# Newton steps of the norms' reciprocal roots: thirteen short chains taken from VectorE to GpSimd

## The chip, the cores and the metric

The program runs on one core of a Trainium2 chip. Time is device time in microseconds (us) from the first to the last instruction of the program, plus a little around it; of several runs the median is given. The engines of the core work side by side, each through its own list of instructions in a fixed order: PE (TensorE, matmuls), PEld (its weight loads), DVE (VectorE), ACT (ScalarE), POOL (GpSimd) and SP (SyncE), which here issues all transfers.

## What is computed

Attention over 4 batches, 12 heads, 448 positions and head size 64, with RMS norms on q and k, followed by two feed-forward layers over 1792 tokens (768 to 2048 to 768 each).

```python
def rmsnorm(x, g):
    rms = np.sqrt(np.mean(x * x, axis=-1, keepdims=True) + 1e-06)
    return x / rms * g
...
q_n, k_n = (rmsnorm(q, g_q), rmsnorm(k, g_k))
scores = scale * np.matmul(q_n, k_n.transpose(0, 1, 3, 2))
...
attn = np.exp(scores)
...
h = x @ w_in
g = h * (1.0 / (1.0 + np.exp(-1.702 * h)))
return (g @ w_out).astype(np.float32)
...
h = x @ w_in
g = np.maximum(h, 0.0) + alpha * np.minimum(h, 0.0)
return (g @ w_out).astype(np.float32)
```

## The kernel before

Two heads make a pair; there are 6 pairs in a batch (`NP`) and 24 in all. Fp32 values are split into two fp16 parts (high and low), and three matmuls of parts stand for one of fp32. The weights come as 64-bit words and are put together, scaled and split on ACT and DVE (`from_words`, lines 132, 148 and 149; row maxima, line 222; splits, lines 163 and 164). `w1i` and `w1o` are the two weights of the first layer.

The head of a pair's work is `normalize` and `prep_pair`. In `normalize`, ACT squares q and k (line 365), DVE sums the squares (line 367) into `ss`, 14 sums per partition and pair, and a reciprocal root `rs` is made from `ss`: one addition (line 368), a seed by integer arithmetic on the bits (line 371), and three Newton steps of three instructions each (lines 375 to 377). These 11 instructions depend on each other in a row. Then q and k are multiplied by the gains (line 382) and by `rs` (line 383), on DVE for the first 8 pairs and on POOL for the other 16. `prep_pair` copies the result to fp16 on ACT (line 396), takes the rest as the low part (line 397, same choice of engine) and has both transposed by a transfer (`hl` to `t1`; for the first pairs `t1` lies in the space of `w1o`). Only then can PE make scores (line 446). `normalize` runs for pair 0, for pair 1, and then for two pairs at once: 13 times in all.

The program starts with half of the work of batch 0 for its 6 pairs (`first_pairs`: scores, exponents, transposes by matmuls on line 493, products with v on line 529), and takes three steps of `w1i` with each of its steps. When the row scales of `w1i` and the scale of v are known, `first_x` splits the attention's output (tile `x`, lines 124 and 125), and the first feed-forward matmuls start (line 624, tile `hp`), mixed with the other half of batch 0 and the steps of `w1o`. Their results go through lines 635 and 636 into `g0`, are split (line 125, tile `g`) and feed the first layer's second product (line 694, tile `yp`), the first of which stands where batch 0 is done. Then the batches follow each other, with the next batch's attention spread between the matmuls, and the second layer comes last.

The order of each engine is not the order of the code: a scheduler simulates the program with its own prices and lists each engine's instructions as they come ready. So short instructions of a dependent row can have others between them, and a change of a few instructions moves many others. SP's list is in order too: a transfer that waits holds up those behind it.

Of the kernel before, what the change touches and what calls it, by code (L numbers as in the profile page):

```python
# [14 lines left out]
ALU = mybir.AluOpType  # L15
# [41 lines left out]
def attention_moe_kernel(  # L57
# [17 lines left out]
    nc = tc.nc  # L75
# [277 lines left out]
    def normalize(*Ps):  # L353

        Ps = [P for P in Ps if P < B * NP]
        if not Ps:
            return
        n = NT2
        w = 2 * n * len(Ps)
        ss = small.tile([128, 4 * NT2], F32, tag="ss", name="ss")[:, 0:w]  # L360
        for t, P in enumerate(Ps):
            flat = raws[P].rearrange("p h c d -> p (h c) d")
            for i in range(2):
                sq = att_p.tile([128, n, D], F32, tag="sq", name="sq", bufs=SQB)
                nc.scalar.activation(out=sq, in_=flat[:, i * n:(i + 1) * n], func=AF.Square, scale=2.0 ** -13)
                o = (2 * t + i) * n
                nc.vector.tensor_reduce(out=ss[:, o:o + n], in_=sq, op=ALU.add, axis=AX)
        nc.vector.tensor_scalar(out=ss, in0=ss, scalar1=1e-6 * 2.0 ** -20, scalar2=None, op0=ALU.add)
        rs = small.tile([128, 4 * NT2], F32, tag="rs", name="rs")[:, 0:w]
        tn = small.tile([128, 4 * NT2], F32, tag="tn", name="tn")[:, 0:w]  # L370
        nc.vector.tensor_scalar(
            out=rs.bitcast(I32), in0=ss.bitcast(I32), scalar1=-0.5, scalar2=RSQRT_SEED, op0=ALU.mult, op1=ALU.add
        )
        for _ in range(3):
            nc.vector.scalar_tensor_tensor(out=tn, in0=rs, scalar=-0.5, in1=ss, op0=ALU.mult, op1=ALU.mult)
            nc.vector.tensor_tensor(out=tn, in0=tn, in1=rs, op=ALU.mult)
            nc.vector.scalar_tensor_tensor(out=rs, in0=tn, scalar=1.5, in1=rs, op0=ALU.add, op1=ALU.mult)
        for t, P in enumerate(Ps):
            side = nc.vector if P < NP + 2 else nc.gpsimd
            ks = raws[P][:, :, 0:4]  # L380
            flat = raws[P].rearrange("p h c d -> p (h c) d")
            side.tensor_tensor(out=ks, in0=ks, in1=gs.unsqueeze(1).to_broadcast([128, 2, 4, D]), op=ALU.mult)
            side.tensor_tensor(
                out=flat, in0=flat, in1=rs[:, 2 * n * t:2 * n * (t + 1)].unsqueeze(2).to_broadcast([128, 2 * n, D]), op=ALU.mult
            )
# [187 lines left out]
    def first_pairs():  # L573

        steps = attention([4 * P + r for P in range(NP) for r in range(2)])
        for i, _ in enumerate(steps):
            P, r = divmod(i, 2)
            if P >= NP:
                yield
                continue  # L580
            if r == 0:
                prep = prep_pair(P + 1) if P + 1 < NP else iter(())
            next(prep, None)
            if r == 0 and P % 2 == 0 and P + 2 < NP:
                normalize(P + 2, P + 3)
            if r == 1:
                if P + 1 + QKB < NP:
                    load_qk(P + 1 + QKB)
                if P + 3 < NP:
                    load_v(P + 3)  # L590
            yield

    def other_batches():
        for i, _ in enumerate(attention(list(range(4 * NP, NU)))):
            P, r = divmod(4 * NP + i, 4)
            if P < B * NP:
                if r == 0:
                    prep = prep_pair(P + 1)
                next(prep, None)
                if r == NORM_AT and P % 2 == 0:  # L600
                    normalize(P + 2, P + 3)
                if r == 2 and P % NP == NP - 2 and P // NP + 1 < B:
                    with tc.issue_after(moved[P].ins):
                        v_scale(P // NP + 1)
                if r == 3:
                    load_qk(P + 1 + QKB)
                    load_v(P + 3)
            yield
# [416 lines left out]
    if True:  # L1025
# [30 lines left out]
        )  # L1056
        next(w1i_steps)
        normalize(0)
        for _ in prep_pair(0):
            pass  # L1060
# [88 lines left out]
```

## Time and profile before

| | |
|---|---|
| median of 3 runs | 1225.83 us (1224.32 to 1228.76) |
| the profiled execution | 1228.48 us, its span 1226.7 us |
| PE busy | 1087.1 us, 89% of the span |
| DVE busy | 842.5 us, 69% |
| ACT busy | 707.7 us, 58% |
| POOL busy | 80.2 us, 7%, 54 instructions |
| mean granted clock of TensorE | 0.960 |

Shares are means over the whole program. A stretch in which one engine is busy all the time while the others idle is limited by that engine, whatever the mean says. A short instruction on DVE is listed with a longer duration than the time it keeps the next one waiting: the start of the next row shows that.

### The profile page before, as it was taken

To read this page: it belongs to the slowest core of one execution; us is meant where nothing else is said; L and a number is where in the kernel's file an instruction comes from. 1 tells how busy PE (TensorE), PEld (TensorE's weight loads), DVE (VectorE), ACT (ScalarE), POOL (GpSimd) and SP (SyncE) were. 2 spreads that over 40 slices of the span, in tenths; PEclk is the share of its full clock that TensorE was granted. 3 is DMA by queue.
4 is the path that set the end of the run, shared out by engine and by line. 5 is a ranking of instruction groups with operands and counts; after the bars stand their busy time and mean duration, and the time that the engine had idled before them with its cause. 6 is when DMAs were issued, how large, how long until landed. Compare 5 with 4: busy or idle time off the path is not lost.

```text
span 1226.7 us, 18612 instructions
## 1 busy us (share of the span) xinstructions
PE 1087.1 (89%) x6829; PEld 608.2 (50%) x6829; DVE 842.5 (69%) x1594; ACT 707.7 (58%) x1447; POOL 80.2 (7%) x54
## 2 busy tenths in 40 slices
PE   0537499967998997999999999799999999999998
PEld 0315277746543443545545545344444467666665
DVE  7998868899656787556662577649896343787451
ACT  3666677878467867558874445227666444565220
POOL 0000000033212221221000000000000000000000
PEclk9966799988999998999999999899999999999999
DMA  7955426566777766655643641266524214354111
GB/s 221 282 155 169 117 54 145 130 124 125 156 146 148 141 135 114 130 127 115 111 99 81 236 157 49 79 235 219 198 89 155 78 65 157 107 160 117 46 32 33
DMA packets 266539, 160.62 MB, mean 131 GB/s; under 512 B 188112, under 2 KB 249808, under 8 KB 266448
## 3 DMA queue, kind: packets, MB, share of 16 engines
q1 hardware_dynamic: 266448, 159.44, 50.1%
q8 instruction: 53, 0.87, 0.3%
q14 instruction: 38, 0.31, 0.1%
HBM read 92.02 MB, written 25.69 MB: 96 GB/s over the span
## 4 chain that ended last, share of the span: by engine, by line
PE 56%; DVE 20%; DMA 11%; ACT 6%; issue 5%; SPq 2%; ACTq 0%; DVEq 0%
PE op L942 16%; PE yp L694 13%; PE hp L671 8%; PE h L779 6%; PE xp L529 5%; PE sp L446 3%; PE hp L624 3%; PE tp L493 2%; DMA yr<-y_dram 2%; DVE nm L451 2%; DVE ph L504 2%; DMA w2raw<-in_moe_w_in_dram 2%; ACT pr L460 1%; DMA vst<-in_v_dram 1%; DVE g L125 1%
## 5 line engine op out<-in xcount | busy, mean ns | idle before, releaser
L694 PE MATMUL yp<-g,w1o 128*128 128x448 f16 x1152 | 231.3, 360 | 5.2 <-DVE t L680 2.3
L779 PE MATMUL h<-x,w2i 128*128 128x512 f16 (+1 forms) x1152 | 219.3, 352 | 3.0 <-ACT neg L786 2.9
L671 PE MATMUL hp<-x,w1i 128*128 128x448 f16 x864 | 171.1, 355 | 3.0 <-DVE t L680 2.3
L694 PEld LDWEIGHTS <-w1o 128*128 128x128 f16 x1152 | 111.8, 99 | 116.9 <-issue 19.9
L779 PEld LDWEIGHTS <-w2i 128*128 128x128 f16 x1152 | 112.6, 98 | 108.6 <-issue 4.0
L671 PEld LDWEIGHTS <-w1i 128*128 128x128 f16 x864 | 82.7, 98 | 86.4 <-issue 12.8
L460 ACT ACTIVATE pr<-sp,nm,c_s 128x448 f32<-128x448 f32 x168 | 120.3, 720 | 4.9 <-PE tp L493 1.6
L504 DVE SCALAR_TENSOR_TENSOR ph<-pr,sm,ph 128x448 f16<-128x448 f32 x126 | 101.7, 831 | 25.0 <-ACT ph L478 24.9
L451 DVE TENSOR_REDUCE nm<-sp 128x2 f32<-128x896 f32 x96 | 92.7, 965 | 4.7 <-PE sp L446 4.4
L446 PE MATMUL sp<-t 64*128 64x448 f16 (+1 forms) x480 | 63.5, 370 | 29.7 <-ACT pr L460 13.5
L942 PEld LDWEIGHTS <-even 128*128 128x128 f16 x672 | 65.7, 98 | 43.1
L478 ACT ACTIVATE ph<-pr,sm 128x448 f16<-128x448 f32 x126 | 77.9, 661 | 14.5 <-DVE sm L469 14.1
L787 DVE SCALAR_TENSOR_TENSOR pos<-neg,nalpha,pos 128x512 f32<-128x512 f32 (+1 forms) x64 | 43.5, 682 | 60.0 <-ACT neg L786 59.9
L785 ACT ACTIVATE pos<-h 128x512 f32<-128x512 f32 (+1 forms) x64 | 34.5, 539 | 69.9 <-PE h L779 58.5
L624 PE MATMUL hp<-x,w1i 128*128 128x256 f16 (+1 forms) x576 | 64.3, 270 | 8.3 <-DVE t L636 7.5
L446 PE MATMUL sp<-w1o 64*128 64x448 f16 (+1 forms) x96 | 16.2, 462 | 62.0 <-DMA w1o<-hl 55.7
L942 PEld LDWEIGHTS <-odd 128*128 128x128 f16 x504 | 49.3, 98 | 32.6
L452 ACT ACTIVATE nm<-nm,c_s 128x2 f32<-128x2 f32 x96 | 28.0, 292 | 63.7 <-DVE nm L451 63.2
L942 PE MATMUL op<-w2lo,even 128*128 128x384 f16 x384 | 63.5, 326 | 0.0
L624 PEld LDWEIGHTS <-w1i 128*128 128x128 f16 x576 | 54.0, 102 | 18.8 <-issue 14.8
L125 DVE SCALAR_TENSOR_TENSOR g<-t,ratio_w1o,g 128x448 f16<-128x448 f32 x64 | 47.2, 741 | 16.0 <-ACT g L124 15.8
L493 PE MATMUL tp<-dg,pr 128*128 128x128 f32 x336 | 51.4, 308 | 5.1 <-DVE dg L473 3.8
(201 smaller groups left out, 1621.0 us busy)
## 6 DMA issues: line engine op xcount, KB each, us to landing
g<-in_moe_w_in_dram SPq DMA_DIRECT2D x24, 512.0 KB, 5.4
g<-in_moe_w_out_dram SPq DMA_DIRECT2D x32, 384.0 KB, 3.5
w2raw<-in_moe_w_in_dram SPq DMA_DIRECT2D x24, 512.0 KB, 5.8
w2raw<-in_moe_w_out_dram SPq DMA_DIRECT2D x16, 768.0 KB, 6.3
g_dram<-pos SPq DMA_DIRECT2D x48, 256.0 KB, 2.0
gp<-g_dram SPq DMA_DIRECT2D x8, 1024.0 KB, 7.6
odd<-g_dram SPq DMA_DIRECT2D x6, 1024.0 KB, 5.8
y_dram<-y SPq DMA_DIRECT2D x24, 224.0 KB, 2.4
```

The costliest lines, as they stand in the source:

```text
L446: nc.tensor.matmul(out=sp[:, j, 0:S] if n == 2 else sp[ds, 0, 0:S], lhsT=qt[ds] if n == 2 else qt[ds, 64:128], rhs=kt[ds, 0:S], start=(i = ...
L451: nc.vector.tensor_reduce(out=nm[:, 0:n], in_=sp[:, 0:n, 0:S], op=ALU.max, axis=AX, negate=True)
L460: nc.scalar.activation(out=pr[i], in_=sp[:, i, 0:S], func=AF.Exp, bias=nm[:, i:i + 1], scale=c_s, accum_out=sm[:, i:i + 1])
L478: nc.scalar.activation(out=ph[:, i, 0:S], in_=pr[i], func=AF.Copy, scale=sm[:, i:i + 1])
L493: nc.tensor.matmul(out=tp[:, c, i], lhsT=pr[i][:, o:o + 128], rhs=ph[:, i], start=True, stop=True)
L504: nc.vector.scalar_tensor_tensor(out=ph[:, i, S:2 * S], in0=pr[i], scalar=sm[:, i:i + 1], in1=ph[:, i, 0:S], op0=ALU.mult, op1=ALU.subtract)
L529: nc.tensor.matmul(out=xp[64 * j:64 * j + 64, t:t + n], lhsT=vs[ks, j, c], rhs=pt[ks, kc, o:o + n], start=(i == 0), stop=(i == len(steps) ...
L624: nc.tensor.matmul(out=ps, lhsT=w1i[:, kk, e, m * 128:(m + 1) * 128], rhs=xs[0, kk][:, f, cols], start=(i == 0), stop=(i == 3 * KD - 1))
L671: nc.tensor.matmul(out=ps, lhsT=w1i[:, kk, e, m * 128:(m + 1) * 128], rhs=x[:, f], start=(n == 0), stop=(n == 3 * KD - 1))
L694: nc.tensor.matmul(out=ps, lhsT=w1o[:, m, e, j * 128:(j + 1) * 128], rhs=g[:, m, f], start=(n == 0), stop=(n == 3 * KF - 1))
L779: nc.tensor.matmul(out=ps, lhsT=w2i[:, kk, e, m * 128:(m + 1) * 128], rhs=x2[kk][:, f], start=(c == 0), stop=(c == 3 * KD - 1))
L942: nc.tensor.matmul(out=ps, lhsT=ops[:, o, m, f], rhs=rhs[:, e], start=(c == 0), stop=(c == 3 * KH - 1))
```

## The change

The 11 instructions on DVE become 14 on POOL. POOL gets the addition and the seed as they are; a Newton step, three instructions with two operations each where that was possible, becomes four with plain products. The number of steps, the tiles and everything around them stay as they were.

```diff
-        nc.vector.tensor_scalar(out=ss, in0=ss, scalar1=1e-6 * 2.0 ** -20, scalar2=None, op0=ALU.add)
+        nc.gpsimd.tensor_scalar(out=ss, in0=ss, scalar1=1e-6 * 2.0 ** -20, scalar2=None, op0=ALU.add)
...
-        nc.vector.tensor_scalar(
+        nc.gpsimd.tensor_scalar(
             out=rs.bitcast(I32), in0=ss.bitcast(I32), scalar1=-0.5, scalar2=RSQRT_SEED, op0=ALU.mult, op1=ALU.add
         )
         for _ in range(3):
-            nc.vector.scalar_tensor_tensor(out=tn, in0=rs, scalar=-0.5, in1=ss, op0=ALU.mult, op1=ALU.mult)
-            nc.vector.tensor_tensor(out=tn, in0=tn, in1=rs, op=ALU.mult)
-            nc.vector.scalar_tensor_tensor(out=rs, in0=tn, scalar=1.5, in1=rs, op0=ALU.add, op1=ALU.mult)
+            nc.gpsimd.tensor_tensor(out=tn, in0=rs, in1=rs, op=ALU.mult)
+            nc.gpsimd.tensor_tensor(out=tn, in0=tn, in1=ss, op=ALU.mult)
+            nc.gpsimd.tensor_scalar(out=tn, in0=tn, scalar1=-0.5, scalar2=1.5, op0=ALU.mult, op1=ALU.add)
+            nc.gpsimd.tensor_tensor(out=rs, in0=tn, in1=rs, op=ALU.mult)
```

The changed code has one line more, so a line behind 377 has a number higher by one in the rows of the change (384 is 383 of before).

DVE's list, before, from the start of the chain for pairs 2 and 3 (`ss` of 28 columns); `w1i` and `g` are weights on their way, `v_95` and `sm`, `dg` belong to v and to the attention of pair 0 and 1:

```order
L368 TENSOR_SCALAR ss<-ss 128x28
L148 TENSOR_SCALAR w1i<-w1i 128x512
L405 TENSOR_REDUCE v_95<-w1o 128x1
L164 SCALAR_TENSOR_TENSOR w1i<-w1i,inv_w1i 128x2048
L371 TENSOR_SCALAR rs<-ss 128x28
L469 RECIPROCAL sm<-sm 128x2
L149 SCALAR_TENSOR_TENSOR w1i<-g_139,w1i 128x512
L148 TENSOR_SCALAR w1i<-w1i 128x512 x2
L375 SCALAR_TENSOR_TENSOR tn<-rs,ss 128x28
L148 TENSOR_SCALAR w1i<-w1i 128x512
L473 TENSOR_SCALAR dg<-identf,sm 128x128 x2
L469 RECIPROCAL sm<-sm 128x2
```

Three of the 11 instructions stand in these rows; the other eight follow in the same manner, and the multiplication by `rs` stands about as many rows behind the last of them. The same place in the change, from the last sum of squares of pair 3 to that multiplication:

```order
L367 TENSOR_REDUCE ss<-sq 128x7
L383 TENSOR_TENSOR qk<-qk,gs 128x2x256
L406 TENSOR_REDUCE v_95<-w1o 128x1
L452 TENSOR_REDUCE nm<-sp 128x2
L156 TENSOR_SCALAR inv_w1i<-rm_w1i 128x1
L148 TENSOR_SCALAR w1i<-w1i 128x512
L470 RECIPROCAL sm<-sm 128x2
L148 TENSOR_SCALAR w1i<-w1i 128x512
L149 SCALAR_TENSOR_TENSOR w1i<-g_139,w1i 128x512
L474 TENSOR_SCALAR dg<-identf,sm 128x128 x2
L149 SCALAR_TENSOR_TENSOR w1i<-g_139,w1i 128x512
L384 TENSOR_TENSOR qk<-qk,rs 128x896 x2
```

Twelve instructions of other work lie between the two now, and the multiplication of pairs 2 and 3 stands ahead of most of the weights.

POOL's list, before, from its first work of the program on:

```order
masks.py:197 MEMSET ident 128x128
masks.py:199 ISA
masks.py:199 AFFINE_SELECT ident<-ident 128x128
L382 TENSOR_TENSOR qk<-qk,gs 128x2x256 x2
L383 TENSOR_TENSOR qk<-qk,rs 128x896 x2
L397 TENSOR_TENSOR hl<-qk,hl 128x896
```

and in the change, the head of the third chain of now, that of pairs 2 and 3 (the last four rows stand there twice more):

```order
L368 TENSOR_SCALAR ss<-ss 128x28
L371 TENSOR_SCALAR rs<-ss 128x28
L375 TENSOR_TENSOR tn<-rs 128x28
L376 TENSOR_TENSOR tn<-tn,ss 128x28
L377 TENSOR_SCALAR tn<-tn 128x28
L378 TENSOR_TENSOR rs<-tn,rs 128x28
```

Five such chains stand on POOL ahead of its first multiplication by `gs`, where nothing stood before.

SP's list, before, around the third transposition (that of pair 2); L200 are loads of weights:

```order
L725 DMA nalpha<-in_moe_alpha_dram 128x16x1
L200 DMA g_139<-in_moe_w_in_dram 128x1024 x9
L200 DMA g_139<-in_moe_w_out_dram 128x4x192
L402 DMA_TRANSPOSE w1o<-hl 128x14x128
L328 DMA qk<-in_k_dram 128x2x192
L329 DMA qk<-in_q_dram 128x2x192
L330 DMA qk<-in_k_dram 64x2x64
```

and the same transposition in the change:

```order
L345 DMA v_547<-in_v_dram 64x2x64
L346 DMA v_547<-in_v_dram 64x2x64
L343 DMA vr<-in_v_dram 128x2x192
L403 DMA_TRANSPOSE w1o<-hl 128x14x128
L328 DMA qk<-in_k_dram 128x2x192
L329 DMA qk<-in_q_dram 128x2x192
L330 DMA qk<-in_k_dram 64x2x64
```

Before, all 24 loads of `w1i` and one of `w1o` were issued ahead of it; in the change 12 loads of `w1i` are, and the others follow behind.

## Rows read from the trace of the kernel before

**Rows 1.** Busy time by stretch: us, PE, PEld, DVE, ACT, POOL, clock, DMA
```profile
16.00:160.00 144.00, 73.65 (x377) 45.52 (x378) 132.39 (x297) 88.69 (x180) 0.00 (x0) 0.80 0.67 188
160.00:250.00 90.00, 90.00 (x699) 64.19 (x699) 70.86 (x170) 69.95 (x178) 2.54 (x2) 1.00 0.46 107
250.00:306.00 56.00, 38.54 (x388) 30.04 (x387) 52.92 (x113) 44.84 (x106) 19.33 (x11) 0.85 0.69 131
306.00:540.00 234.00, 215.35 (x1437) 107.73 (x1437) 156.11 (x316) 153.10 (x356) 48.30 (x31) 0.96 0.70 138
540.00:1226.00 686.00, 669.60 (x3936) 360.68 (x3934) 423.06 (x671) 347.16 (x625) 9.37 (x5) 1.00 0.39 119
...
160.00:169.40 9.40, 9.40 (x65) 5.82 (x64) 5.22 (x16) 8.10 (x24) 0.00 (x0) 1.00 0.01 3
```

**Rows 2.** Who waited for whom, PE, from 16 to 160: us, times, longest
```profile
PE sp L446 <- DMA w1o<-hl: 55.7, 4, 25.7
```

**Rows 3.** Timeline of DVE, pairs 2 and 3: start us, us, instruction
```profile
34.44 0.17 DVE L368 TENSOR_SCALAR ss<-ss 128x28 f32<-128x28 f32 x1
...
70.15 0.18 DVE L377 SCALAR_TENSOR_TENSOR rs<-tn,rs 128x28 f32<-128x28 f32 x1
...
72.19 2.09 DVE L383 TENSOR_TENSOR qk<-qk,rs 128x896 f32<-128x896 f32 x2
...
80.24 1.09 DVE L397 TENSOR_TENSOR hl<-qk,hl 128x896 f16<-128x896 f32 x1
```

**Rows 4.** Groups of DVE instructions by line and shape: busy us, mean ns
```profile
L377 DVE SCALAR_TENSOR_TENSOR rs<-tn,rs 128x28 f32<-128x28 f32 x33 | 6.0, 183 | 0.5
...
L164 DVE SCALAR_TENSOR_TENSOR w1o<-w1o,inv_w1o 128x768 f16<-128x768 f32 x14 | 13.8, 1013 | 0.0
...
L149 DVE SCALAR_TENSOR_TENSOR w1o<-g,w1o 128x384 int32<-128x384 int32 x28 | 15.2, 552 | 0.0
...
L222 DVE TENSOR_REDUCE rm_w1o<-w1o 128x1 f32<-128x768 f32 x14 | 13.3, 948 | 0.1
...
L148 DVE TENSOR_SCALAR w1o<-w1o 128x384 int32<-128x384 int32 x28 | 9.8, 355 | 6.9 <-ACT w1o L132 6.6
```

**Rows 5.** Timeline of DVE, the first chain (pair 0)
```profile
8.27 0.16 DVE L368 TENSOR_SCALAR ss<-ss 128x14 f32<-128x14 f32 x1
...
11.30 0.23 DVE L260 TENSOR_TENSOR gq<-gq,gk 128x64 f32<-128x64 f32 x1 [2.65 <-DMA gk<-in_g_k_dram]
...
14.59 0.16 DVE L377 SCALAR_TENSOR_TENSOR rs<-tn,rs 128x14 f32<-128x14 f32 x1
14.67 0.61 DVE L367 TENSOR_REDUCE ss<-sq 128x7 f32<-128x448 f32 x1
15.20 0.68 DVE L382 TENSOR_TENSOR qk<-qk,gs 128x512 f32<-128x512 f32 x1
15.80 1.09 DVE L383 TENSOR_TENSOR qk<-qk,rs 128x896 f32<-128x896 f32 x1
```

**Rows 6.** Timeline of DVE: the sixth split of x, and the last split of g
```profile
169.40 0.48 DVE L125 SCALAR_TENSOR_TENSOR x<-xraw,first_sc,x 128x256 f16<-128x256 f32 x1
...
312.92 0.68 DVE L125 SCALAR_TENSOR_TENSOR g<-t,ratio_w1o,g 128x448 f16<-128x448 f32 x1
```

**Rows 7.** Timeline of POOL, its first instructions
```profile
0.34 0.10 POOL L1133 MEMSET const-uint8-127<- 128x1 uint8 x1
0.73 0.20 POOL masks.py:197 MEMSET ident<- 128x128 bf16 x1 [0.29 <-POOLq L1133]
1.01 0.29 POOL masks.py:199 TENSOR_SCALAR_AFFINE_SELECT ident<-ident 128x128 bf16<-128x128 bf16 x1
237.60 1.27 POOL L382 TENSOR_TENSOR qk<-qk,gs 128x512 f32<-128x512 f32 x1 [236.29 <-ACT sm L464]
```

**Rows 8.** Lines 382 and 383 by engine: shortest/median/longest ns, first and last start
```profile
L382 POOL TENSOR_TENSOR qk<-qk,gs x16: 1262/1268/1371, 237.6 to 535.7; 128x512 f32<-128x512 f32 x16
...
L383 POOL TENSOR_TENSOR qk<-qk,rs x16: 1687/1690/2069, 255.5 to 541.6; 128x896 f32<-128x896 f32 x16
...
L383 DVE TENSOR_TENSOR qk<-qk,rs x8: 1079/1086/1091, 15.8 to 148.2; 128x896 f32<-128x896 f32 x8
```

## The prediction

> **What bounds the kernel now.** I read the busy time by stretch first [rows 1]. From 540 on PE is busy 669.6 of 686 us, and from 160 to 250 it is busy all the time: there nothing but matmuls counts. From 16 to 160 it is the other way round: PE has 73.7 us of work in 144 us, while DVE is busy 132.4 us, 92%, and idles 11.6 us. From 250 to 306 DVE is busy 52.9 of 56 us and PE 38.5. So the first 160 us and the last 56 us of batch 0 go at the pace of DVE's list, and what shortens the list up to a certain instruction, or lets PE's work fit beside it, is worth time there.
>
> The waits of PE in the first stretch show what the list does to it [rows 2]: 55.7 us of its idle time are four waits for the transposed `hl` of a pair. The timeline of DVE says why for pair 2 [rows 3]: the chain of 11 short instructions starts at 34.44 and its last one at 70.15, so 36 us go by for instructions of 0.18 us, since the scheduler put weights between them. The multiplication follows at 72.19, the low part at 80.24. PE sits idle for it, but DVE doesn't: it does weights that are needed later anyway. The reader should keep both apart: the latency of the chain costs PE idle time that is no loss while DVE is the bound, and DVE's own time in the chain is small.
>
> **The change, part by part.** *DVE loses work.* A chain instruction lasts 0.16 to 0.18 us, but the next row starts earlier: 14.59 to 14.67 in the first chain, 0.08 us, and some 0.1 us with 28 columns, where the next but one depends on it [rows 4, 5]. I take 0.09. All 13 chains are 143 instructions, 13 us of DVE's list. Ahead of the sixth split of `x`, without which the first `hp` can't be finished, stand five chains, 55 instructions: 5.0 us.
>
> *Other work moves behind that point.* I counted DVE's lists up to the sixth split of `x`: 342 instructions before, 270 in the change. 55 of the 72 are chains; the other 17 are work on `w1o`: 4 splits at 1.01 us, 4 and 3 of lines 149 and 148 at 0.55 and 0.36, one maximum at 0.95, five of one column at about 0.07 [rows 4]. With the overlap of 0.08 us that rows 5 show between neighbours (15.20 to 15.80 for an instruction of 0.68) that is 3.7 + 1.9 + 0.8 + 0.9 + 0.4 = 7.7 us. So the sixth split stands 12.7 us earlier in the list; before it started at 169.40 [rows 6].
>
> *The idle time of DVE up to there.* It was 11.6 us from 16 to 160 [rows 1], which I keep. From 160 to 169.4, where PE was busy all the time and DVE idle for 4.2 of 9.4 us [rows 1], the change has DVE work of `w1o` to do, and PE's attention is done earlier: worth 0 to 4 us; I take 2, as PE's own order up to the first `hp` is the same. The first `hp` group then is complete some 15 us earlier.
>
> *What is given back.* PE's order from there to the end of batch 0 is nearly the same, and PE was busy 90 of 90 us, so it follows the shift. DVE gets the 7.7 us of `w1o` back in this stretch. It idles 19 of these 90 us [rows 1], so most of it fits: 0 to 7.7, I take 2. As a check, up to the last split of `g`, which started at 312.92 [rows 6], DVE's list is shorter by 76 chain instructions, 6.8 us, and longer by two low parts of `ph` and a few others, net 5 us; the rest of the gain must come from idle time that goes. That is the weak step of this sum. From 306 to 540 there are 67 more chain instructions, 6 us of DVE, which isn't the bound there (156 of 234 us busy); PE idles 18.7 us [rows 1]. Worth 0 to 6; I take 1. Behind 540 nothing.
>
> *POOL gets 14 dependent instructions per chain.* The trace has none of this size. From below: a fill of one column is 0.10 us; from the multiplication's 1.69 us for 896 columns, through zero, 28 columns are 0.05 us [rows 7, 8]. From above: a line through lines 382 and 383 (1.262 us for 512, 1.687 for 896) leaves 0.70 us at no columns and 0.73 at 28 [rows 8]. Between dependent instructions lie 0.08 us (0.73 + 0.20 to 1.01 [rows 7]). So an instruction costs 0.10 to 0.81 us. Nearest in kind is the selection of 128 columns, 0.29 us, and the fill of 0.20: I take 0.25, 3.5 us per chain (1.4 to 11.3).
>
> What hides it is DVE's work between the last sum of squares and the multiplication, which waits in DVE's list with everything queued behind it. For pairs 2 and 3 these are the twelve instructions in the order shown with the change: 4.6 us. For pair 0 POOL can start at 8.27, and the gains arrive at 11.30 and take until 13.8 [rows 5]: 5.5 us. For pair 1, and for 4 and 5, 6 and 7, likewise 4.0, 7.5 and 9.4. A chain of 3.5 us is hidden five times; at 5.6 us (0.40 each) 2.7 us of stalls begin to show. From pair 8 on the multiplication is on POOL itself, busy 48.3 of 234 us [rows 1]: hidden.
>
> The Trainium skill, page "GPSIMD Engine Reference", section "Performance versus the Vector engine", calls GpSimd the wrong choice for ordinary elementwise work, about half as fast. The trace agrees on large tiles: line 383 takes 1.69 us on POOL and 1.09 on DVE [rows 8]. By its 2.6 cycles per element at 1.2 GHz, 28 columns would be 0.06 us beside the dispatch, as an estimate. By that alone the chains would be hidden too; what decides here is the fixed part, for which the rows above give the bounds.
>
> *SP.* The third transposition stood behind all 24 loads of `w1i`, and now stands behind 12; the loads behind it wait for `hl` of pair 2, which comes at about 45 instead of 80. No term of its own.
>
> **Sum.** 12.7 + 2 - 2 + 1 = 13.7 us less, and I take 0.7 off for stalls at an instruction of 0.33 us in place of 0.25, as POOL's spans are rough: 13. The profiled execution is 1228.48, 2.7 above the median; the runs' median less 13 is 1213 us, with a range of its own of 1208 to 1219.
>
> **The rivals.** *Idle time goes too.* PE's attention is no longer behind, so DVE's short waits shrink as well: of 11.6 + 4.2 us another 6 to 10 go. For it: PE idles 70 us from 16 to 160. Against it: DVE is 92% busy there. 1204 (1200 to 1208).
>
> *The gain is paid back before batch 0 ends.* The 7.7 us of `w1o` come back in full, since DVE is the bound from 250 to 306, and only the 5 us of the last split of `g` stay, or less: 1222 (1219.7 to 1226). For it: DVE's 95% there. Against it: 19 us of DVE idle ahead of it.
>
> *The chains on POOL are long.* If an instruction costs 0.65 us, a chain is 9.1 us, and DVE stalls 3.6 + 5.1 + 4.5 + 1.6 = 15 us at its multiplications, more than the gain; at 0.81 it is 25 us. 1228 to 1239, slower from 0.6 us an instruction. For it: the line through the two large shapes. Against it: a selection of 128 columns with its fixed part is 0.29 us.
>
> *The first chain is cold.* If POOL's first arithmetic at 8.3 starts late by more than 2 us, pair 0's multiplication stalls DVE by the rest. Against it: the first multiplication at 237.60 took 1.27 us, as the others did [rows 7, 8]; a delay of 6 us would give 1217. The same skill page, section "Instruction dispatch", states about 6 us for the first call to freshly loaded code; no row here shows one.
>
> **How the numbers follow.** Forecast 0.50, idle time too 0.17, paid back 0.19, long chains 0.11, cold 0.03. What a measurement of this kernel can tell from no change is about 0.5%, 6.1 us: below 1219.7 or above 1231.9. Faster is the forecast, the second and the last, less a little of the forecast's edge: 0.68. Same is "paid back" and the lower third of the long chains: 0.23. Slower is the rest: 0.09. The range leaves out the best half of the second case and the slow end: 1203 to 1229.
>
> **What would show it.** DVE with 143 instructions less. The multiplication of pairs 2 and 3 near 37 in place of 72, the sixth split of `x` near 155, the first `yp` near 293 in place of 306, and the last 686 us as before. POOL's instructions of 28 columns at 0.2 to 0.35 us, with no wait of DVE's line 384 for `rs` above 1 us. The prediction is wrong if such waits are several us each, or if the first `hp` comes 13 us earlier and the first `yp` doesn't.

## The result and the profile after

The change takes 1211.29 us (median of 4 runs, 1210.01 to 1213.63); the kernel before 1227.3 us (median of 4 runs, 1224.32 to 1231.59, the three given with its profile among them). The ratio is 0.987, with a 95% interval of 0.983 to 0.990: faster by 1.3%. The profiled execution has a span of 1208.2 us, 18.5 less than the one of before.

The busy line of the page of the change: DVE has 1451 instructions, POOL 236 in place of 54.

```profile
PE 1086.0 (90%) x6829; PEld 610.5 (51%) x6829; DVE 827.2 (68%) x1451; ACT 704.2 (58%) x1447; POOL 138.7 (11%) x236
```

The first stretch of [rows 1] in the change (columns as there, the last one is GB/s):

```profile
16.00:160.00 144.00, 95.61 (x535) 62.81 (x536) 133.74 (x275) 100.16 (x221) 21.54 (x56) 0.88 0.69 189
```

In its first 160 us PE now does 95.6 us of work where it did 73.7 [rows 1], with DVE as busy as it was. For the gain I cut both traces at the same instruction instead of the same time: at the sixth split of `x`, at the first `yp`, and at the first matmul of line 671 (672 in the change), batch 1's `hp`. Ahead of the last one stand 1973 matmuls in both kernels (the views count 1973 or 1974 by where the cut falls), so that it is a cut at the same work of PE too; ahead of the other two the change has 12 and 21 matmuls more. Of the kernel before, in the columns of the view above:

```profile
16.00:169.40 153.40, 83.05 (x440) 51.34 (x440) 137.61 (x311) 96.79 (x204) 0.00 (x0) 0.81 0.63 177
169.40:306.00 136.60, 119.14 (x1021) 88.40 (x1020) 118.57 (x267) 106.69 (x260) 21.87 (x13) 0.94 0.58 124
0.00:388.30 388.30, 277.07 (x1974) 177.76 (x1975) 313.39 (x718) 257.65 (x587) 39.89 (x30) 0.90 0.63 152
```

and of the change:

```profile
16.00:148.60 132.60, 85.24 (x452) 55.23 (x452) 124.11 (x249) 91.95 (x200) 21.54 (x56) 0.87 0.71 193
148.60:288.90 140.30, 120.00 (x1030) 88.72 (x1029) 125.95 (x266) 109.91 (x266) 30.08 (x42) 0.93 0.60 135
0.00:370.80 370.80, 279.00 (x1973) 180.72 (x1974) 306.66 (x621) 257.96 (x594) 81.27 (x156) 0.92 0.65 159
```

The sixth split comes 20.8 us earlier, the first `yp` 17.1, line 672 17.5. Behind that point both kernels need the same time: 1226.7 - 388.3 = 838.4 us and 1208.2 - 370.8 = 837.4. So the gain lies ahead of batch 1's feed-forward, all of it in PE's idle time: 388.3 - 277.1 = 111.2 us before, 370.8 - 279.0 = 91.8 now, 19.4 less, while PE's work takes 1.9 us more.

For whom PE waited, in PE's groups up to that matmul. First the kernel before (busy, mean ns of one, then idle time ahead of the group and for whom):

```profile
L624 PE MATMUL hp<-x,w1i 128*128 128x256 f16 (+1 forms) x576 | 64.3, 270 | 8.3 <-DVE t L636 7.5 <-DVE g L636 0.8
L493 PE MATMUL tp<-dg,pr 128*128 128x128 f32 x336 | 51.4, 308 | 5.1 <-DVE dg L473 3.8 <-ACT ptf L499 1.3
L446 PE MATMUL sp<-t 64*128 64x448 f16 (+1 forms) x216 | 30.2, 384 | 24.5 <-DMA t<-hl 10.5 <-ACT pr L460 8.3 <-ACT nm L452 5.6
L446 PE MATMUL sp<-w1o 64*128 64x448 f16 (+1 forms) x96 | 16.2, 462 | 62.0 <-DMA w1o<-hl 55.7 <-ACT pr L460 6.2
```

and the change:

```profile
L625 PE MATMUL hp<-x,w1i 128*128 128x256 f16 (+1 forms) x576 | 64.8, 271 | 11.5 <-DVE t L637 8.0 <-DVE x L125 1.2 <-DVE g L637 1.0
L494 PE MATMUL tp<-dg,pr 128*128 128x128 f32 x336 | 56.1, 326 | 15.4 <-DVE dg L474 14.9 <-DVE mv L120 0.5
L447 PE MATMUL sp<-t 64*128 64x448 f16 (+1 forms) x216 | 29.7, 375 | 12.1 <-ACT pr L461 12.1
L447 PE MATMUL sp<-w1o 64*128 64x448 f16 (+1 forms) x96 | 16.2, 434 | 41.9 <-DMA w1o<-hl 38.5 <-ACT pr L461 3.4
```

The two groups of scores, which wait for `hl`, idle 86.5 us before and 54.0 now: 32.5 less, of which the waits put down to `hl` itself are 27.7 (66.2 before, 38.5 now). The two groups above them take 13.5 of that back, 10.3 of it the transposes, which now wait 14.9 us for `dg` (3.8 before). `dg` comes from DVE: what got earlier was paid for partly by what got later in the same list.

One such place, in DVE's timeline of the change (start, duration, instruction):

```profile
39.44 2.09 DVE L384 TENSOR_TENSOR qk<-qk,rs 128x896 f32<-128x896 f32 x2 [1.08 <-POOL rs L378]
41.45 2.35 DVE L164 SCALAR_TENSOR_TENSOR w1i<-w1i,inv_w1i 128x2048 f16<-128x2048 f32 x1
43.72 1.08 DVE L452 TENSOR_REDUCE nm<-sp 128x2 f32<-128x896 f32 x1
...
46.64 0.16 DVE L470 RECIPROCAL sm<-sm 128x2 f32<-128x2 f32 x1
46.72 1.12 DVE L367 TENSOR_REDUCE ss<-sq 128x7 f32<-128x448 f32 x2
...
50.29 0.48 DVE L474 TENSOR_SCALAR dg<-identf,sm 128x128 f32<-128x128 f32 x2
```

and the row of PE's timeline that belongs to it:

```profile
50.63 3.78 PE L494 MATMUL tp<-dg,pr 128*128 128x128 f32 x16 [8.04 <-DVE dg L474]
```

The multiplication that began at 72.19 [rows 3] is at 39.44. But the maximum `nm` stands behind it and a split of weights, and `dg` stands behind sums and gains of later pairs, another maximum and two steps of weights, 3.65 us after its reciprocal began. PE waits 8 us for it, with the next scores already done.

### The profile page after: what moved, and what is told of

Read it like the earlier page. It is cut to its first block, busy times and chain, and to the rows that moved or that the text cites. A ratio compares the mean times of both kernels' runs of the same rounds, so it can differ in the third digit from the quotient of the medians.

```text
span 1208.2 us, 18626 instructions
## 1 busy us (share of the span) xinstructions
PE 1086.0 (90%) x6829; PEld 610.5 (51%) x6829; DVE 827.2 (68%) x1451; ACT 704.2 (58%) x1447; POOL 138.7 (11%) x236
## 4 chain that ended last, share of the span: by engine, by line
PE 49%; DVE 21%; DMA 12%; ACT 9%; issue 5%; SPq 3%; POOL 0%; DVEq 0%; ACTq 0%
PE op L943 13%; PE yp L695 10%; PE h L780 9%; PE hp L672 7%; PE xp L530 4%; DVE ph L505 3%; ACT pr L461 3%; DMA w2raw<-in_moe_w_in_dram 2%; PE sp L447 2%; DVE nm L452 2%; PE hp L625 2%; DMA vst<-in_v_dram 2%; PE tp L494 2%; DMA yr<-y_dram 1%; DMA w2raw<-in_moe_w_out_dram 1%
## 5 line engine op out<-in xcount | busy, mean ns | idle before, releaser
L505 DVE SCALAR_TENSOR_TENSOR ph<-pr,sm,ph 128x448 f16<-128x448 f32 x126 | 104.9, 857 | 30.9 <-ACT ph L479 30.2
L494 PE MATMUL tp<-dg,pr 128*128 128x128 f32 x336 | 56.1, 326 | 15.4 <-DVE dg L474 14.9
L494 PEld LDWEIGHTS tp<-dg,pr 128*128 128x128 f32 x336 | 49.8, 230 | 26.9 <-DVE dg L474 11.8
```

Of the source, the lines that this page charges most:

```text
L494: nc.tensor.matmul(out=tp[:, c, i], lhsT=pr[i][:, o:o + 128], rhs=ph[:, i], start=True, stop=True)
L505: nc.vector.scalar_tensor_tensor(out=ph[:, i, S:2 * S], in0=pr[i], scalar=sm[:, i:i + 1], in1=ph[:, i, 0:S], op0=ALU.mult, op1=ALU.subtract)
```

## The experiments

Twelve kernels ran in three groups of four, each group on one chip beside runs of the kernel before, whose medians there are 1226.68, 1226.85 and 1225.37 us. All compute the whole output. The theories: that the *load* counts (what leaves DVE's list is gained; theory 1 of the expectations), that the *latency* or place of the chains counts (their end, wherever they run; theory 2), that GpSimd itself matters, in the later batches too (theory 3), and, later, that the *order* which the scheduler makes counts.

**1. Chains on DVE, but close together.** In the kernel before, the steps of `w1i` in each part of `first_pairs` may only issue behind that part's chain.

```diff
-            nc.vector.scalar_tensor_tensor(out=rs, in0=tn, ...)
+            root[0] = nc.vector.scalar_tensor_tensor(out=rs, in0=tn, ...)
...
-            for _ in range(W_RATE):
-                next(w1i_steps, None)
+            with tc.issue_after(root[0].ins):
+                for _ in range(W_RATE):
+                    next(w1i_steps, None)
```

> The chains stay on VectorE, 11 instructions each, but the steps of w1i that the code issues after a chain may not be listed ahead of its end, so that the chain of pairs 2 and 3 stands in some 28 rows of VectorE's list instead of 90. VectorE has all its 143 instructions. Theory 1 (VectorE's list got shorter: its own chain time, 5 to 7 us up to the end of batch 0, is most of the gain): 1218 to 1222 us, a third of the gain. Theory 2 (place: what counts is that pairs 2 to 5 are normalized early, ahead of the weights, whichever engine does it): 1210 to 1215 us. Theory 3 (GpSimd itself matters, also in the later batches): 1225 us, as before.

1226.32 us, ratio 1.000 (0.998 to 1.002). PE's groups up to line 672 show the trade:

```profile
L494 PE MATMUL tp<-dg,pr 128*128 128x128 f32 x336 | 55.6, 325 | 16.8 <-DVE dg L474 14.6 <-ACT ptf L500 1.1 <-DVE g L637 1.1
L530 PE MATMUL xp<-pt,vs 128*64 128x256 f16 (+1 forms) x264 | 21.5, 300 | 18.7 <-DMA pt<-ph 13.3 <-DVE x L125 3.8 <-DVE ph L505 1.6
...
L447 PE MATMUL sp<-w1o 64*128 64x448 f16 (+1 forms) x96 | 14.4, 421 | 41.6 <-DMA w1o<-hl 29.0 <-ACT pr L461 12.6
```

That is the time of theory 3, and of neither of the other two. The waits for `hl` fell as in the change, so for the first pairs latency can be had on DVE, but `dg` and `pt` got late. In the profiled execution PE's idle time up to line 672 is 12.2 us less than before and its work 6.5 more; the 5.7 us that this leaves are taken up behind that line (844.2 us where it was 838.4, table below), and the medians show nothing of them. `hl` of pairs 2 to 5 comes 2 to 7 us later than in the change, that of pair 6 at 141.4 in place of 106.6. The rule itself may cost something; experiment 7 looks at that.

**2. The load put back, latency kept.** The change, and beside each chain on POOL the same 11 instructions once more on DVE, into tiles `dr` and `dn` that nobody reads.

```diff
+        dr = small.tile([128, 4 * NT2], F32, tag="dr", name="dr")[:, 0:w]
+        dn = small.tile([128, 4 * NT2], F32, tag="dn", name="dn")[:, 0:w]
+        nc.vector.tensor_scalar(out=dn, in0=ss, ...)
+        nc.vector.tensor_scalar(out=dr.bitcast(I32), in0=ss.bitcast(I32), ...)
+        for _ in range(3):
+            nc.vector.scalar_tensor_tensor(out=dn, in0=dr, scalar=-0.5, in1=ss, ...)
+            nc.vector.tensor_tensor(out=dn, in0=dn, in1=dr, op=ALU.mult)
+            nc.vector.scalar_tensor_tensor(out=dr, in0=dn, scalar=1.5, in1=dr, ...)
```

> The change as it is, and beside it VectorE also does its old 11 instructions of each chain on two tiles that nobody reads: VectorE gets its load back, without anyone waiting for it. Theory 1 (load): the 5 to 7 us up to the end of batch 0 come back, 1216 to 1219 us. Theory 2 (place): 1210 to 1213 us, as the change.

1218.44 us, 0.994 (0.992 to 0.997): about half of the gain goes, as theory 1 said. By 0.09 us each, the 143 instructions are 13 us of DVE's list, and 7 us of time came back. The second chain also reads `ss`, which has two buffers, and `hl` of pair 2 comes at 50.85 in place of 45.64. Whether the load or the held buffers make it late, no run parts, so this loss need not be the load's alone.

**3 and 4. The first five chains on POOL alone, and the last eight alone** (with `>=` in place of `<`); the other chains stay on DVE as before.

```diff
+        if Ps[0] < NP + 2:
+            nc.gpsimd.tensor_scalar(out=ss, in0=ss, ...)
...
+        else:
+            nc.vector.tensor_scalar(out=ss, in0=ss, ...)
...
```

> Only the five chains of pairs 0 to 7 are on GpSimd, the other eight on VectorE as before. Theories 1 and 2: nearly all of the gain, 1210 to 1215 us. Theory 3 (the later chains count too, 6 us of VectorE from 306 to 540): 1217 us or more.

> Only the eight chains of pairs 8 to 23 are on GpSimd, the first five on VectorE as before. Theories 1 and 2: 1223 to 1227 us, no change that can be told. Theory 3: 1219 to 1221 us.

The first five: 1212.92 us, 0.990 (0.988 to 0.992). The last eight: 1222.15 us, 0.996 (0.994 to 0.998). The first is as theories 1 and 2 had it; the second lies between what they gave and what theory 3 gave. Together 1.0% + 0.4%, about what the change has. In experiment 4 PE's idle time up to line 671 is 381.6 - 271.0 = 110.6 us, as before; its work is shorter, by 6.1 us, for the same matmuls. What made it shorter is not settled by any run here; two profiles of the same kernel differ by up to 2.5 us in this number (the change and 9 in the table below).

**5. Longer chains.** Six Newton steps in place of three on POOL: 26 instructions per chain.

```diff
-        for _ in range(3):
+        for _ in range(6):
```

> Six Newton steps on GpSimd instead of three: 26 dependent instructions per chain, some 7.8 us instead of 4.2. If the chain's length on GpSimd is hidden (the scheduler puts other work of VectorE ahead of the multiplication), 1211 to 1215 us. If it is not, the first three chains each add up to 3.6 us of stalls to a list that is the bound: 1219 to 1224 us.

1209.83 us, 0.987 (0.985 to 0.990): as the change. POOL's work rises by 56 us, and DVE's waits for `rs` up to 160 us stay where they were (4.0 us in three waits; 3.6 in two in the change): the multiplications moved back in the list (`hl` of pair 2 at 56.9 instead of 45.6). The sixth split of `x` comes at 158.0, 9.4 us later than in the change, and the end is the same. So the length of a chain doesn't count at this size, and that landmark isn't the bound I took it for. DVE is busy some 9 us less than in the change up to line 672 (table below), and the time is the same.

**6 and 10. The first two chains back on DVE**, the other eleven on POOL; twice, in two groups. The two chains carry a priority too (`tc.high_priority`), so that the scheduler lists them ahead of other work that is ready: engine and place change together.

```diff
+        if Ps[0] >= 2:
+            nc.gpsimd.tensor_scalar(out=ss, in0=ss, ...)
...
+        else:
+            with tc.high_priority():
+                nc.vector.tensor_scalar(out=ss, in0=ss, ...)
...
```

> The chains of pairs 0 and 1 are back on VectorE, 22 instructions, the other eleven stay on GpSimd. The wait of VectorE of 2.5 us for the chain of pair 1 goes, and 2 us of load come. If waits and load weigh the same: 1210 to 1213 us, as the change. If the place of the two first chains among the weights matters most: 1215 us or more.

> The sixth experiment once more, to see whether it beats the change on the same chip. If it does: 3 to 6 us less than the change. If the first result was chance: the same as the change within 2 us.

1206.28 us, 0.984 (0.981 to 0.987), and 1202.61 us, 0.982 (0.980 to 0.984): the best version. Both of the first expectations are missed, and the second time the gain on the change is 9.1 us (experiment 9, same chip), more than the 3 to 6 I gave. PE's groups of the second one, up to line 683 (671 of before), at 364.2:

```profile
L636 PE MATMUL hp<-x,w1i 128*128 128x256 f16 (+1 forms) x576 | 63.7, 270 | 3.0 <-ACT ptf L511 1.7 <-DVE g L648 0.8 <-DVE t L648 0.5
L505 PE MATMUL tp<-dg,pr 128*128 128x128 f32 x336 | 51.5, 311 | 6.1 <-DVE dg L485 3.2 <-ACT ptf L511 2.8
L458 PE MATMUL sp<-t 64*128 64x448 f16 (+1 forms) x216 | 28.2, 373 | 17.4 <-ACT pr L472 17.3
L458 PE MATMUL sp<-w1o 64*128 64x448 f16 (+1 forms) x96 | 14.3, 424 | 54.7 <-DMA w1o<-hl 40.4 <-ACT pr L472 14.3
```

The scores wait 72.1 us, more than in the change (54.0), and `dg` and `t` are in time again. PE's timeline at the place of the change's wait of 8 us:

```profile
45.14 3.96 PE L505 MATMUL tp<-dg,pr 128*128 128x128 f32 x24
```

The scores of pair 1 start at 42.79 here and at 35.73 in the change. But the first 32 transposes are done at 53.1 us here (24 in one go, as shown, and 8 from 51.93) and at 54.4 in the change, whose second 16 wait for `dg` until 50.63. So up to there, to be early with pair 1 was worth nothing. DVE's waits for `rs` sum to 1.1 us here. PE's idle time is the same as in the change (364.2 - 272.1 = 92.1); its work is shorter by 6.9 us, 4.6 of it the transposes (by 4.4 and 3.2 beside the second profile of the change, experiment 9).

**7. The rule of experiment 1, nearly, on the change**: the steps of `w1i` issue behind the last sum of squares (in 1 it was behind the end of the chain).

```diff
-                nc.vector.tensor_reduce(out=ss[:, o:o + n], in_=sq, op=ALU.add, axis=AX)
+                root[0] = nc.vector.tensor_reduce(out=ss[:, o:o + n], in_=sq, op=ALU.add, axis=AX)
...
+            with tc.issue_after(root[0].ins):
```

> The change, with the rule of the first experiment on the list: the steps of w1i that the code issues after a normalization may not be listed ahead of its last sum of squares. It tells whether that rule itself, not the engine of the chains, took the gain of the first experiment. If the rule costs: 1216 us or more. If it does not: 1210 to 1214 us, and what the first experiment lacked is VectorE's shorter list.

1216.5 us, 0.993 (0.991 to 0.996). The rule costs some 5 to 8 us by itself. Under it the chains on POOL are still 0.7% ahead of chains on DVE (experiment 1), as far as the two rules are the same.

**8, 11 and 12. Other load off DVE.** The multiplications and low parts go to POOL from pair 4 on instead of pair 8: in the change (8), in the kernel before (11), and in version 6 (12).

```diff
-            side = nc.vector if P < NP + 2 else nc.gpsimd
+            side = nc.vector if P < 4 else nc.gpsimd
...
-        (nc.vector if P < NP + 2 else nc.gpsimd).tensor_tensor(out=hl[:, 1], ...)
+        (nc.vector if P < 4 else nc.gpsimd).tensor_tensor(out=hl[:, 1], ...)
```

> The change, and pairs 4 to 7 are multiplied and split on GpSimd too (three large instructions each, 12 in all), as the later pairs are: VectorE loses 11 us more of its list up to the end of batch 0. Load theory: 5 to 9 us faster than the change, 1202 to 1207 us. If GpSimd's slower work makes the pairs late instead: 1211 us or more.

> The kernel before, all its chains on VectorE, with pairs 4 to 7 multiplied and split on GpSimd: VectorE loses 11 us in the first 160 us, more than the five chains there cost it, but the chain of pairs 2 and 3 is as spread out as before. Load theory: 1217 to 1221 us. Place theory (pairs 2 and 3 late, whatever VectorE has to do): 1223 to 1228 us.

> The sixth experiment and the eighth together. If the list of VectorE is again filled with other weights in the time that comes free, as in the eighth: 1206 to 1210 us. If it is not: 1200 to 1204 us.

1212.41 us, 0.989 (0.987 to 0.991); 1238.33 us, 1.010 (1.008 to 1.013); 1205.52 us, 0.984 (0.982 to 0.986). Load's 1202 to 1207 for 8 did not come; 11 is slower than either expectation, and 12 lies between its two. Four pairs are 4 x (0.68 + 1.09 + 1.08) = 11 us of DVE. The change gained nothing from losing them, and the kernel before got slower. Its groups say where (up to 370 us):

```profile
L493 PE MATMUL tp<-dg,pr 128*128 128x128 f32 x336 | 51.4, 305 | 14.0 <-DVE dg L473 9.5 <-ACT ptf L499 4.5
...
L446 PE MATMUL sp<-w1o 64*128 64x448 f16 (+1 forms) x96 | 15.9, 463 | 58.6 <-DMA w1o<-hl 58.6
```

`hl` as late as it was, and `dg` later. With 8, DVE's list up to the sixth split of `x` has 274 instructions, where the change has 270: work on `w1o` moved into the room.

But these runs don't test the load theory as they were meant to. Up to batch 1's `hp`, DVE is busy only 3.3 us less in 8 than in the change, and 0.2 less in 11 than before (table below), though 11 us of instructions left. Others got longer beside POOL's large multiplications. Line 149 on `w1o`, first in the change, then in 8:

```profile
L149 DVE SCALAR_TENSOR_TENSOR w1o<-g,w1o 128x512 int32<-128x512 int32 x8 | 5.4, 678 | 0.0
L149 DVE SCALAR_TENSOR_TENSOR w1o<-g,w1o 128x512 int32<-128x512 int32 x8 | 9.3, 1186 | 0.0
```

The last section has rows of the same in the change. What these runs do show is that instructions taken off DVE are not load taken off DVE when POOL's replacements are large.

**9. The change once more**, in the group of 10 to 12.

> The change itself, beside the three others of this call, so that they are compared on the same chip: 1209 to 1214 us.

1211.75 us, 0.989 (0.987 to 0.991), as expected; 10 beats it with intervals apart.

The first matmul of batch 1's `hp` (1973 ahead of it), and what PE and DVE did until then, in us; "behind" is the span behind it:

| | at | PE busy | PE idle | behind | DVE busy |
|---|---|---|---|---|---|
| before | 388.3 | 277.1 | 111.2 | 838.4 | 313.4 |
| the change | 370.8 | 279.0 | 91.8 | 837.4 | 306.7 |
| 1 tight chains on DVE | 382.6 | 283.6 | 99.0 | 844.2 | 313.6 |
| 2 both engines | 382.7 | 282.4 | 100.3 | 835.3 | 317.9 |
| 3 first five | 369.2 | 279.1 | 90.1 | 840.7 | 305.9 |
| 4 last eight | 381.6 | 271.0 | 110.6 | 837.2 | 313.1 |
| 5 six steps | 374.7 | 273.1 | 101.6 | 835.9 | 297.9 |
| 6 two on DVE | 364.9 | 270.6 | 94.3 | 837.4 | 309.7 |
| 7 the rule on the change | 383.9 | 285.2 | 98.7 | 834.8 | 310.6 |
| 8 more on POOL | 372.2 | 280.2 | 92.0 | 838.8 | 303.4 |
| 9 the change again | 371.9 | 276.5 | 95.4 | 842.2 | 307.5 |
| 10 two on DVE again | 364.2 | 272.1 | 92.1 | 836.0 | 309.4 |
| 11 before, more on POOL | 395.2 | 282.0 | 113.2 | 834.8 | 313.2 |
| 12 two on DVE, more on POOL | 369.5 | 277.6 | 91.9 | 835.1 | 304.4 |

The change and 9 are one kernel, as are 6 and 10: their profiles differ by up to 3.6 us in idle time, 2.5 in work and 4.8 behind, so smaller differences say nothing. Behind this matmul all lie within 9.4 us, which is not much beyond that; ahead of it they spread over 31.0. The three kernels with the five chains of batch 0 spread over DVE's list (before, 4, 11) have 111 to 113 us of idle time, all others 90 to 102.

DVE's load goes with the result in the large: the six kernels with 310.6 us or more come to this matmul at 381.6 or later, the eight with less at 374.7 or earlier. In the small it doesn't: of the eight, 5 has the least load and is the last, and 6 and 10 have the most and are the first.

## Why the prediction was right, and where its steps were off

The forecast of 1213 us with its range of 1208 to 1219 held. By its steps:

*The list up to the sixth split of `x`, 12.7 us less.* Right as a count. From 16 us on DVE was busy 137.6 us up to it and is 124.1 now: 13.5 less. But the step from there to the end, that the end follows this landmark, isn't borne out: in experiment 5 the sixth split comes 9.4 us later than in the change, and the time is the same.

*Idle time of DVE up to there, 2 us less, at most 4.* Too small: it was 153.4 - 137.6 = 15.8 us and is 132.6 - 124.1 = 8.5, so 7.3 less. The rival "idle time goes too" was right about this stretch, though not about the end: the 20.8 us were not all kept.

*Given back, 2 us, 0 to 7.7.* From the sixth split to the first `yp` the change takes 140.3 us where it took 136.6: 3.7 given back. The rival that all of it is paid back didn't come about. The form was the one I described: `w1o` comes back. DVE is busy 126.0 us in this stretch where it was busy 118.6, 7.4 more although two chains have left it (by the view of tile `w1o` alone, 37.2 us where it was 28.6), and it idles 14.3 us in place of 18.0, so about half of it fits. PE's waits for `dg`, 14.9 us, all lie ahead of the sixth split; they are a price inside the 20.8 us, not a part of this term.

*Later chains, 1 us.* Experiment 4, where only these move, gives 0.36% (0.17 to 0.56), 4.4 us, within the 0 to 6 that I gave, but not from PE's waits, which I had named as its source.

*POOL's chain hidden five times, no wait above 1 us.* Mis-sized. The instruction I took at 0.25 us, at 0.33 with reserve. Alone it is that: from one start to the next 0.30 us, 0.31 with 28 columns. But of the 154 instructions of 28 columns, which I had expected at 0.2 to 0.35 us, 29 last longer, the longest 3.11 us. POOL's timeline of the change, first chain and start of the second:

```profile
7.92 0.27 POOL L368 TENSOR_SCALAR ss<-ss 128x14 f32<-128x14 f32 x1 [6.63 <-DVE ss L367]
...
11.84 0.22 POOL L378 TENSOR_TENSOR rs<-tn,rs 128x14 f32<-128x14 f32 x1
16.01 0.63 POOL L368 TENSOR_SCALAR ss<-ss 128x14 f32<-128x14 f32 x1 [3.95 <-DVE ss L367]
16.72 0.21 POOL L371 TENSOR_SCALAR rs<-ss 128x14 int32<-128x14 int32 x1
17.01 1.51 POOL L375 TENSOR_TENSOR tn<-rs 128x14 f32<-128x14 f32 x1
18.60 0.66 POOL L376 TENSOR_TENSOR tn<-tn,ss 128x14 f32<-128x14 f32 x1
...
19.68 0.66 POOL L378 TENSOR_TENSOR rs<-tn,rs 128x14 f32<-128x14 f32 x1
...
22.50 0.22 POOL L378 TENSOR_TENSOR rs<-tn,rs 128x14 f32<-128x14 f32 x1
```

Pair 0's chain takes 7.92 to 12.06, 4.1 us, or 0.30 per instruction from start to start, and is hidden by its cover of 5.5. The start isn't cold: 0.27 us for the first instruction. Pair 1's takes 16.01 to 22.72, 6.7 us, since four instructions last 0.63 to 1.51 us, and its cover was 4.0. DVE in the same time:

```profile
15.84 0.68 DVE L383 TENSOR_TENSOR qk<-qk,gs 128x512 f32<-128x512 f32 x1
16.44 0.68 DVE L406 TENSOR_REDUCE v<-w1o 128x1 f32<-128x512 f32 x1
17.03 1.08 DVE L398 TENSOR_TENSOR hl<-qk,hl 128x896 f16<-128x896 f32 x1
18.03 0.42 DVE L148 TENSOR_SCALAR w1i<-w1i 128x512 int32<-128x512 int32 x1
18.49 0.69 DVE L149 SCALAR_TENSOR_TENSOR w1i<-g,w1i 128x512 int32<-128x512 int32 x1
...
19.57 0.69 DVE L149 SCALAR_TENSOR_TENSOR w1i<-g,w1i 128x512 int32<-128x512 int32 x1
22.75 1.09 DVE L384 TENSOR_TENSOR qk<-qk,rs 128x896 f32<-128x896 f32 x1 [2.49 <-POOL rs L378]
```

Each long one on POOL ends just behind a DVE instruction with two tensor inputs: 16.64 behind 16.52, 19.26 behind 19.18, 20.34 behind 20.26; the one of 1.51 us ends at 18.52, behind 18.11 and the instruction of one input after it. The one of 0.21 us at 16.72 lies beside an instruction with one input, and those from 20.42 on beside none. (One of pair 0, at 11.24, keeps its 0.22 us beside a product of only 64 columns.) So DVE waited 2.49 us for pair 1 and 1.08 for pairs 2 and 3 (the row at 39.44 further up; eleven instructions cover that chain, not the twelve of the forecast), 3.6 in all, where the sum had 0.7. Experiment 6 took the first two chains off POOL, and with them the wait of 2.5.

*What would show it.* 143 instructions less on DVE: 1451 now, 1594 on the page of before. The multiplication of pairs 2 and 3 near 37: 39.4. The sixth split near 155: 148.6. The first `yp` near 293: 288.9. The end as before: 838.4 and 837.4 us behind line 671. The bound on the waits failed, and with it the one on the length of POOL's instructions.

So the sum up to the first `yp`, where 12.7 + 2 - 2 - 0.7 = 12.0 us were forecast, came to 13.5 + 7.3 - 3.7 = 17.1, with the waits for `rs` inside DVE's idle time. The term that was mis-sized is that idle time. Behind the first `yp` another 1.4 us came, where 1 was forecast. That makes 18.5 in the spans, where 13 were forecast; the medians of the result differ by 16.0. So the forecast of 1213 us, 1.7 off, is better than its steps, and that is partly luck: the median of the kernel before was 1.5 us higher in the result than in the forecast, the profiled pair shows 5.5 us more than the sum, and the sum goes by a landmark that experiment 5 moves without effect.

What is the cause, then? The runs show that it is neither DVE's load alone (against it are 5, where DVE is busy some 9 us less than in the change and the time is the same, and 6 and 10, where it is busy some 3 us more and the time is 5 to 9 us less) nor the chains' end alone (5 again, where `hl` of pair 2 comes 11 us later). But load isn't out of it: in 2, where it was put back, half of the gain went, and the table above parts the kernels by it. With the chains on DVE, `hl` of pair 2 and later pairs stood behind most of the weights; without them the scheduler makes another order, in which PE's scores wait 32.5 us less, 27.7 of it for `hl`, and some 14 us more is waited for what stands behind. That is shown for the change by the groups above. That another order would gain more is shown by 6 and 10, but why is argued only: the early scores of pair 1, the later `dg`, and PE's shorter work go together there, and no run parts them. How much of 2 is load and how much the held buffers is open too. Nor does a run part DVE's new order from SP's, whose loads of weights moved behind the transpositions. And the nearest rival wasn't tried: all chains on DVE as a strict sequence, with the priority that 6 gives to two of them and no other rule. So that the chains had to leave DVE for this gain is not shown.

## What to carry to other kernels

Small dependent instructions that a scheduler spreads through a full list can delay their reader by many times their own time (36 us for 11 instructions [rows 3]); to move them to an idle engine makes a new order too, so read for whom the bounding engine waits afterwards, group by group, and cut both traces at the same instruction count rather than the same time. A landmark halfway is no forecast of the end: the sixth split moved by 9 us between the change and experiment 5 with no effect. When a move pays, try it for a part: here two of the thirteen chains, left on DVE with priority, gained another 5 to 9 us. And when work goes from one engine to another, sum up the busy time of the first one again: 11 us of instructions taken off DVE lowered it by 3.3 and 0.2 us (8 and 11).

## What the runs showed of the hardware

GpSimd's small instructions cost 0.21 to 0.22 us at 14 columns and 0.21 to 0.25 at 28, with some 0.08 us to the next dependent one, and beside VectorE's instructions of two tensor inputs many of them last 0.5 to 1.5 us, one 3.11 us. The Trainium skill, page "GPSIMD Engine Reference", section "Specifications", says that GpSimd shares its SBUF interfaces with VectorE and contends with its instructions of two SBUF inputs. The trace agrees: that is the kind of instruction beside which the four long ones lie.

VectorE shows nothing of these four: its products beside them take 0.68, 1.08 and twice 0.69 us (rows in the section before last), and the same ones elsewhere 0.68 (at 47.76), 1.08 (at 45.64) and 0.68 (at 52.35). Beside GpSimd's large multiplications it pays itself. In the change, with the same product once ahead of two of them and once beside them:

```profile
229.35 0.67 DVE L505 SCALAR_TENSOR_TENSOR ph<-pr,sm,ph 128x448 f16<-128x448 f32 x1
...
230.83 3.34 POOL L384 TENSOR_TENSOR qk<-qk,rs 128x896 f32<-128x896 f32 x2
...
232.49 2.16 DVE L505 SCALAR_TENSOR_TENSOR ph<-pr,sm,ph 128x448 f16<-128x448 f32 x1
```

GpSimd's pair ends at 234.17, and VectorE's second product 0.48 us behind it.

TensorE's work of the same 1973 matmuls takes 270.6 to 285.2 us in the table. The granted clock can be a part of it. In the change 16 transposes take 3.78 us at 50.63, where PE had waited 8 us, and 2.05 at 79.43, behind other matmuls (stretches of the change, columns as above):

```profile
37.57:41.35 3.78, 3.78 (x18) 3.56 (x20) 2.70 (x4) 3.28 (x7) 1.51 (x5) 1.00 0.95 251
50.63:54.41 3.78, 3.78 (x18) 3.56 (x20) 3.78 (x9) 1.88 (x3) 0.00 (x0) 0.50 0.78 174
79.43:81.48 2.05, 2.05 (x17) 1.93 (x17) 2.05 (x2) 1.57 (x4) 0.00 (x0) 1.00 0.81 251
```

The granted clock is 0.50 (1.2 GHz) in the one stretch and 1.00 (2.4 GHz) in the other. The first row, 3.78 us at a granted 1.00, doesn't fit that, so the clock alone doesn't explain every length. From 16 to 160 us the mean is 0.80 before [rows 1] and 0.88 in the change, and yet PE's work up to batch 1's `hp` is 1.9 us longer there: no gain from the clock shows in these two profiles.
